# Moving one of the three u-computations of a slot behind the next W1 in a conv + low-rank mixer kernel

## The chip, the cores and the metric

The kernel runs on one core of a Trainium2 chip. The metric is the device time in microseconds of one execution; "before" is the median of three runs. A core has five engines that run side by side and wait for each other with semaphores: TensorE (PE in the profile, its weight loads PEld), VectorE (DVE), ScalarE (ACT), GpSimd (POOL) and SyncE (SP), which here only issues DMAs. TensorE writes its results to PSUM, which has eight banks of 128 x 512 floats; VectorE or ScalarE must copy a result out before its bank can be used again.

## The reference

The input x is 8 x 4224 x 192 (batch, sequence, channel). First comes a causal convolution with 7 taps along the sequence, with one set of taps, after a softmax, for each of 8 heads of 24 channels:

```python
w = np.exp(weight - weight.max(-1, keepdims=True)); w /= w.sum(-1, keepdims=True) + 1e-9
y[b, s, h, g] = sum_k w[h, k] * x_pad[b, s + k, h, g]
```

Then, with y as the x of the mixer:

```python
xt = x.transpose(0, 2, 1)
h = xt @ U @ V                       # rank 32, along the sequence
u = x + h.transpose(0, 2, 1)
ch = np.maximum(u @ w_ch1, 0.0) @ w_ch2   # 192 -> 768 -> 192
return (u + ch).astype(np.float32)
```

U and V mix along the whole sequence of a batch, so nothing of u of a batch can be had before the conv of that batch is done.

## The kernel before, in words

The 8 x 33 tiles of 128 sequence positions are handled in 33 groups of eight tiles (`NG`, `GT`). A group does not respect batches: batch b is tiles 33b to 33b + 32. The steps are:

- **conv** of a batch (`conv32` from batch 2 on, L317; `conv` before, L351): matmuls of x with banded matrices (L335 or L365), head by head, two PSUM banks a head, copied to `y_sb` by `evac` (ScalarE L252, VectorE L254). The string of letters (`AAD`, `AD`) says which engine makes which copy in turn.
- **t** (`tt_mm`, `tt_split`) and **s** (`tt_sum`): y times U, summed, to `tt_sb`.
- **h** of a group (`h_group`, `h_tiles`, L442): eight matmuls of `tt_sb` with V (L453), two tiles of a pair to one PSUM bank, and then on VectorE the adds u = y + h (L475) from PSUM to `u_sb`. A group that starts on an odd tile of its batch, or runs over the edge of two batches, has five banks and six shorter and longer adds rather than four of one kind. Behind the adds, `transp` issues a transposing DMA on SP's queue (L494), which makes `uT` of the group.
- **W1** of a group (`w1`, L538): 36 matmuls (L550) from `uT` with the first weight, six chunks m of two banks each, and behind each chunk two ReLUs out of PSUM to `rl_sb`, on ScalarE (L564) or VectorE (L566): seven and five per group.
- **W2** of two tiles (`w2`, L573; "a pair" below): 12 matmuls (L579) from `rl_sb` with the second weight to one bank, an add of u on VectorE to `out_sb` (L588) and a DMA to the output on SP's queue (L596).

All PSUM tiles come from one pool of eight banks under one tag. `out_sb` has eight buffers, `u_sb` seven, `uT` five.

The order is written out by hand: the kernel runs under a manual schedule, and every engine executes its instructions in the order in which the code issues them. `SLOTS` (L615) is the list of slots, counted from 0 here. A slot is W1 of its groups in the first list, then the W2 pairs of the groups in the second list, four pairs a group; the dictionary says what is done ahead of which pair ("position"; a slot of three groups has positions 0 to 12):

```python
for gs1, gs2, at in SLOTS:
    for g in gs1: ends = w1(g, ...)
    for p in range(npc + 1):
        for what in at.get(p, []): do(what)
        if p < npc: w2(g, 2 * k, 2)
```

From slot 5 on both lists are the same three groups, and in the slot u of three later groups is made. In slots 5 to 9 there is also the conv of a batch (positions 2 to 4 in slot 5, positions 1 to 3 in slots 6 to 9: three heads, three heads, two heads), t and s. Slots 10 to 12 have three h at positions 0, 4 and 8, and slot 13 has none.

GpSimd loads x (L79) during W1 of groups in `LOADS` (L666), held back to chosen W1 matmuls, and makes a shifted copy of x for the conv (`x_shift`, L282: L289, L291 and L301).

Of the kernel before, what the change touches and what calls it, by code (L numbers as in the profile page):

```python
# [14 lines left out]
def kernel(  # L15
# [40 lines left out]
    def bank():  # L56
        return psp.tile([P, 512], F32, name="ps", tag="ps")
# [192 lines left out]
    def evac(eng, out, in_):  # L250
        if eng == "A":
            nc.scalar.activation(out=out, in_=in_, func=ACT.Copy)  # L252
        else:
            nc.vector.tensor_copy(out=out, in_=in_)  # L254
# [27 lines left out]
    def x_shift(b):  # L282


        xbt[b] = xbs.tile([P, NB1, D], BF16, name="xb_sb")

        def same(s0, s1, *rest):
            def step():
                nc.gpsimd.tensor_copy(out=xbt[b][:, s0:s1, :], in_=xt[b][:, s0 + 1 : s1 + 1, :])  # L289
                for t0, t1 in rest:  # L290
                    nc.gpsimd.tensor_copy(  # L291
                        out=xbt[b][HB : HB + QB, t0:t1, :],
                        in_=xt[b][HB : HB + QB, t0 + 1 : t1 + 1, :],
                    )

            return step

        def ahead(r, s0, s1):
            def step():
                q = slice(HB * r + QB, HB * r + HB)  # L300
                nc.gpsimd.tensor_copy(out=xbt[b][q, s0:s1, :], in_=xt[b][q, s0:s1, :])  # L301

            return step

        m = NB0 // 2
        return [
            same(0, m),
            same(m, NB0, (NB0, NB1)),
            ahead(0, 0, m),
            ahead(0, m, NB0),  # L310
            ahead(1, 0, m),
            ahead(1, m, NB1),
        ]
# [3 lines left out]
    def conv32(b, h0, nh, engs):  # L317


        if yt[b] is None:  # L320
            yt[b] = ys.tile([P, NT, D], BF16, name="y_sb")
        nk = (NB0 // 2, NB1 // 2)
        for n in range(nh):
            h = h0 + n
            hs = slice(h * GS, h * GS + GS)
            pp = [bank(), bank()]
            for cg in range(4):
                t, w, st = (
                    (xt[b], bands[h // HQ][:, h % HQ, QB : 2 * QB], 1 + cg // 2)
                    if cg % 2  # L330
                    else (xbt[b], band2[:, h, :], cg // 2)
                )
                for r in range(2):
                    hr = slice(HB * r, HB * r + HB)
                    nc.tensor.matmul(  # L335
                        out=pp[r][QB * cg : QB * cg + QB, 0 : nk[r] * GS],
                        lhsT=w[hr],
                        rhs=t[hr, st : st + 2 * nk[r] - 1 : 2, hs],
                        start=True,
                        stop=True,  # L340
                        tile_position=(HB * r, QB * cg),
                    )
            for part in range(2):
                j0 = NB0 // 2 * part
                evac(
                    engs[(2 * n + part) % len(engs)],
                    yt[b][:, j0 : j0 + nk[part], hs],
                    pp[part][:, 0 : nk[part] * GS].rearrange("p (k a) -> p k a", a=GS),
                )

    def conv(b, h0, nh, rs, engs, k0=0, k1=NT, pp=None):  # L351

        if yt[b] is None:
            yt[b] = ys.tile([P, NT, D], BF16, name="y_sb")
        nk = {r: min(k1, (NB0, NB1)[r] // 2) - k0 for r in rs}
        if pp is None:
            pp = {r: bank() for r in rs}
        w = nh * GS
        for hh in range(nh):
            h = h0 + hh  # L360
            for halo in range(2):
                for r in rs:
                    for c in range(2):
                        st = 1 - halo + c + 2 * k0
                        last = nc.tensor.matmul(  # L365
                            out=pp[r][HB * c : HB * c + HB, 0 : nk[r] * w].rearrange(
                                "p (k a) -> p k a", a=w
                            )[:, :, hh * GS : hh * GS + GS],
                            lhsT=bands[h // HQ][
                                HB * r : HB * r + HB, h % HQ, HB * halo : HB * halo + HB  # L370
                            ],
                            rhs=xt[b][
                                HB * r : HB * r + HB,
                                st : st + 2 * nk[r] - 1 : 2,
                                h * GS : h * GS + GS,
                            ],
                            start=(halo == 0),
                            stop=(halo == 1),
                            tile_position=(HB * r, HB * c),
                        )  # L380
        for n, r in enumerate(rs):
            j0 = NB0 // 2 * r + k0
            evac(
                engs[n % len(engs)],
                yt[b][:, j0 : j0 + nk[r], h0 * GS : h0 * GS + w],
                pp[r][:, 0 : nk[r] * w].rearrange("p (k a) -> p k a", a=w),
            )
        return last
# [95 lines left out]
    def h_group(g):  # L484
        t0, t1 = g * GT, g * GT + GT
        while t0 < t1:
            b = t0 // NT
            te = min(t1, (b + 1) * NT)
            h_tiles(b, t0 - b * NT, te - b * NT)
            t0 = te  # L490

    def transp(g):
        uTt[g] = uts.tile([P, 4, 3, P], BF16, name="uT")
        return nc.sync.dma_start_transpose(  # L494
            out=uTt[g][:].rearrange("p i c t -> p (i c) t"),
            in_=ut[g][:].rearrange("p i c f k -> p (i c f k)"),
        )
# [100 lines left out]
    def held(ins, after):  # L598
        tc.add_manual_dep(
            ins.ins,  # L600
            after.ins.name,
            mybir.DependencyInfo(mybir.DependencyClass.Sync, mybir.DependencyReason.DATA),
            reason="transfer held back",
        )

    def x_load(b, q, after):
        if q == 0:
            x_tile(b)
            x_zero(b, nc.gpsimd)
        held(x_part(b, *XP[q]), after)  # L610
# [17 lines left out]
                6: ["t2"],  # L628
                8: ["s2"],
                9: ["h8"],  # L630
                11: ["h9"],
            },
        ),
    ]
    nh = 10
    for k in range(5, 14):
        gs = list(range(3 * k - 9, 3 * k - 6))
        hs = [f"h{g}" for g in range(nh, min(nh + 3, NG))] + [None] * 3
        nh = min(nh + 3, NG)
        if k == 5:  # L640
            at = {
                2: ["c3:0:3:AAD"],
                3: ["c3:3:3:AAD"],
                4: ["c3:6:2:A", "x4:3"],
                5: [hs[0]],
                6: ["t3"],
                8: ["s3", hs[1]],
                11: [hs[2]],
            }
        elif k < 10:  # L650
            b = k - 2
            at = {
                1: [f"c{b}:0:3:AAD"],
                2: [f"c{b}:3:3:AAD"],
                3: [f"c{b}:6:2:A"] + ([f"x{b + 1}:3"] if b + 1 < B else []),
                5: [f"t{b}", hs[0]],
                7: [f"s{b}"],
                8: [hs[1]],
                11: [hs[2]],
            }  # L660
        else:
            at = {0: [hs[0]], 4: [hs[1]], 8: [hs[2]]}
        SLOTS.append((gs, gs, {p: [w for w in what if w] for p, what in at.items()}))
# [92 lines left out]
    def do(what):  # L756
        if what[0] == "c":
            b, h0, n, engs = what[1:].split(":")
            conv32(int(b), int(h0), int(n), engs)
            return  # L760
        if what[0] == "d":
            for h in range(H):
                last = conv(int(what[1:]), h, 1, [0, 1], "AA" if h == 2 else "AD")
            held(transp(3), last)
            return
        if what[0] == "l":
            b, q = (int(v) for v in what[1:].split(":"))
            x_load(b, q, done_w2[-1])
            return
        if what[0] == "x":  # L770
            b, n = (int(v) for v in what[1:].split(":"))
            steps.extend(x_shift(b))
            for _ in range(n):
                steps.pop(0)()
            return
        n = int(what[1:])
        if what[0] == "h":
            h_group(n)
            if n > 1 and n != 3:
                transp(n)  # L780
        elif what[0] == "t":
            tt_split(n, tt_mm(n, range(NT)))
        else:
            tt_sum(n)
# [55 lines left out]
```

## Time and profile before

| | us |
|---|---|
| runs | 325.15, 325.98, 326.2 (median 325.98) |
| profiled execution | 325.15 |
| its span, first to last instruction | 323.4 |
| granted TensorE clock (share of full speed) | 0.999 |
| PE, DVE, ACT, POOL busy | 318.0, 269.0, 170.5, 143.5 |
| W1 matmuls (L550), ReLUs of ACT and DVE | 131.7; 124.3 and 105.3 |
| W2 matmuls (L579), output adds (L588) | 141.9; 70.3 |
| u adds (L475), 168 instructions | 66.2 |

Where the slots lie, by the start of their W1 in the chain that ended last: slot 4 at 56.4, slot 5 at 81.1, then 109.4, 137.5, 165.8, 193.9, 222.0, 246.9, 271.8, and slot 13 at 296.4 us. A row of a timeline reads: start, duration, engine, line, operation, what it writes and reads, how many instructions are merged in the row, and in brackets the idle time before and what ended it. A row of the chain reads: start, length, and what the end of the kernel hung on in that stretch; "issue" is time for which the profile shows no wait. The duration of a matmul (246 ns of one at L579) is longer than the distance of two of them, since they are pipelined; distances of starts tell the pace.

### The profile page before, as it was taken

The page shows a single profiled execution, that of the slowest core. Times are in us where ns is not written, and L with a number is a line of the kernel's source. Part 1 is how long each engine was busy: PE and PEld are TensorE (multiplying, and loading weights), DVE is VectorE, ACT ScalarE, POOL GpSimd, SP SyncE. Part 2 cuts the span into 40 slices and gives each one's busy share as a digit, 9 for nine tenths or more (in the row PEclk, how much of TensorE's full clock was granted, in tenths as well). Part 3 has the DMA queues.
Part 4 walks back from the last instruction along what each step waited for, and adds up shares of the span by engine and source line. Part 5 has one row for each costly group of instructions (what it writes and reads, how often), then busy time and mean ns, then how long its engine had stood idle before and what let it go on. Part 6 is the DMA issues. An engine that isn't in the chain of part 4 may idle for free.

```text
span 323.4 us, 9590 instructions
## 1 busy us (share of the span) xinstructions
PE 318.0 (98%) x3998; PEld 223.8 (69%) x3998; DVE 269.0 (83%) x551; ACT 170.5 (53%) x344; POOL 143.5 (44%) x112
## 2 busy tenths in 40 slices
PE   8999999999999999999999999999999999999996
PEld 3757676478677647866864784587797497487495
DVE  7769989987977986998798699879888897896864
ACT  1766724860874397088339708824903902912920
POOL 8684179728957694786859489000000000000000
PEclk9999999999999999999999999999999999999999
DMA  9999993999999899699799957139269059048035
GB/s 104 192 192 177 211 213 99 183 196 263 206 126 214 226 176 171 171 152 201 169 240 131 229 160 195 35 111 245 56 168 272 3 149 264 29 121 270 2 119 176
DMA packets 122907, 53.52 MB, mean 166 GB/s; under 512 B 87760, under 2 KB 122832, under 8 KB 122864
## 3 DMA queue, kind: packets, MB, share of 16 engines
q1 hardware_dynamic: 84528, 38.08, 47.5%
q0 software_dynamic: 38192, 14.73, 40.0%
q8 instruction: 31, 0.51, 0.7%
q10 hardware_dynamic: 144, 0.10, 0.1%
q14 instruction: 12, 0.10, 0.1%
HBM read 29.49 MB, written 25.95 MB: 171 GB/s over the span
## 4 chain that ended last, share of the span: by engine, by line
PE 94%; ACT 3%; DVE 2%; issue 0%
PE ps L579 42%; PE ps L550 39%; PE ps L335 3%; PE ps L453 3%; PE ps L155 2%; PE ps L398 2%; ACT rl_sb L564 2%; PE ps L365 1%; ACT y_sb L252 1%; DVE u_sb L475 1%; DVE rl_sb L566 1%; PE ps L520 0%; PE ps L505 0%; DVE band L254 0%; PE ps L678 0%; PE ps L424 0%
## 5 line engine op out<-in xcount | busy, mean ns | idle before, releaser
L564 ACT ACTIVATE rl_sb<-ps 128x512 bf16<-128x512 f32 x233 | 124.3, 604 | 108.0 <-PE ps L550 96.0
L579 PE MATMUL ps<-W_sb,rl_sb 128*128 128x192 bf16 x1584 | 141.9, 246 | 0.2
L579 PEld LDWEIGHTS <-rl_sb 128*128 128x128 bf16 x1584 | 128.1, 98 | 13.5 <-issue 13.1
L550 PE MATMUL ps<-uT,W_sb 64*128 64x512 bf16 x1188 | 131.7, 376 | 0.0
L566 DVE TENSOR_SCALAR rl_sb<-ps 128x512 bf16<-128x512 f32 x163 | 105.3, 687 | 15.7 <-PE ps L550 15.4
L550 PEld LDWEIGHTS <-W_sb 64*128 64x128 bf16 x1188 | 66.8, 94 | 60.6 <-issue 3.8
L588 DVE TENSOR_TENSOR out_sb<-ps,u_sb 128x384 f32<-128x384 f32 (+1 forms) x133 | 70.3, 548 | 25.9 <-PE ps L579 25.5
L301 POOL COPY xb_sb<-x_sb 32x3072 bf16<-32x3072 bf16 (+1 forms) x24 | 67.5, 2824 | 0.7
L475 DVE TENSOR_TENSOR u_sb<-y_sb,ps 128x192 bf16<-128x192 bf16 (+1 forms) x168 | 66.2, 459 | 0.0
L289 POOL COPY xb_sb<-x_sb 128x3072 bf16<-128x3072 bf16 x12 | 32.7, 2742 | 36.2 <-DMA x_sb<-in_x_dram 22.3
L252 ACT ACTIVATE y_sb<-ps 128x384 bf16<-128x384 f32 (+4 forms) x90 | 38.2, 515 | 10.4 <-PE ps L335 7.8
L79 POOL DMA_DIRECT2D x_sb<-in_x_dram x32 | 27.0, 848 | 17.2 <-PE ps L550 10.3
L254 DVE CAST y_sb<-ps 128x408 bf16<-128x408 f32 (+4 forms) x36 | 19.2, 577 | 0.8 <-PE ps L365 0.7
L453 PE MATMUL ps<-tt_sb,V_sb 32*128 32x192 bf16 x264 | 12.4, 246 | 0.1
L335 PE MATMUL ps<-xb_sb,band 64*32 64x384 bf16 x192 | 12.1, 332 | 0.0
L335 PE MATMUL ps<-x_sb,band 64*32 64x384 bf16 x192 | 12.1, 333 | 0.0
L453 PEld LDWEIGHTS <-V_sb 32*128 32x128 bf16 x264 | 4.7, 92 | 7.3 <-issue 7.3
L155 PE MATMUL ps<-zz 128*128 128x512 f32 x12 | 7.6, 786 | 1.5 <-DVE zz L145 1.5
L365 PE MATMUL ps<-x_sb,band 64*64 64x240 bf16 (+3 forms) x192 | 7.9, 276 | 0.4 <-DVE band L254 0.4
L412 ACT ACTIVATE tt_hi<-ps 128x192 bf16<-128x192 f32 x8 | 2.6, 330 | 10.6 <-PE ps L398 10.5
L335 PEld LDWEIGHTS <-band 64*32 64x32 bf16 x384 | 4.5, 89 | 4.1 <-issue 3.0
L365 PEld LDWEIGHTS <-band 64*64 64x64 bf16 x192 | 5.9, 106 | 2.2 <-issue 1.2
(65 smaller groups left out, 72.7 us busy)
## 6 DMA issues: line engine op xcount, KB each, us to landing
out_dram<-out_sb SPq DMA_DIRECT2D x131, 192.0 KB, 2.8
x_sb<-in_x_dram POOLq DMA_DIRECT2D x14, 384.0 KB, 7.8
x_sb<-in_x_dram POOLq DMA_DIRECT2D x7, 432.0 KB, 8.5
x_sb<-in_x_dram POOLq DMA_DIRECT2D x7, 408.0 KB, 9.0
x_sb<-in_x_dram POOLq DMA_DIRECT2D x1, 504.0 KB, 7.4
uT<-u_sb SPq DMA_TRANSPOSE x31, 3.7
x_sb<-in_x_dram POOLq DMA_DIRECT2D x1, 480.0 KB, 5.7
W_sb<-in_moe_w_ch_dram POOLq DMA_DIRECT2D x2, 192.0 KB, 7.6
```

What stands on the lines that cost most here:

```text
L79: return nc.gpsimd.dma_start(out=xt[b][HB * r : HB * r + HB, s0:s1, :], in_=x[b, blk * HB : (blk + s1 - s0) * HB, :].rearrange("(j p) d -> ...
L252: nc.scalar.activation(out=out, in_=in_, func=ACT.Copy)
L289: nc.gpsimd.tensor_copy(out=xbt[b][:, s0:s1, :], in_=xt[b][:, s0 + 1 : s1 + 1, :])
L301: nc.gpsimd.tensor_copy(out=xbt[b][q, s0:s1, :], in_=xt[b][q, s0:s1, :])
L335: nc.tensor.matmul(out=pp[r][QB * cg : QB * cg + QB, 0 : nk[r] * GS], lhsT=w[hr], rhs=t[hr, st : st + 2 * nk[r] - 1 : 2, hs], start=True, ...
L453: nc.tensor.matmul(out=banks[pr][:, a * D : (a + 1) * D], lhsT=V_sb[32 * q : 32 * q + 32, (j // 8) * 2 + j % 2, :], rhs=ttb[b][32 * q : 32 ...
L475: nc.vector.tensor_tensor(out=u_group(g)[:, i : i + n, :, hf, :], in0=yt[b][:, run[0] : run[0] + n, :].rearrange("p n (c k) -> p n c k", c=3),
L550: last = nc.tensor.matmul(out=pps[m][hf][:], lhsT=W1_sb[HB * hf : HB * hf + HB, c, m * P : (m + 1) * P], rhs=uTt[g][HB * hf : HB * hf + HB ...
L564: nc.scalar.activation(out=rl[:, m, hf, :], in_=pp[hf][:], func=ACT.Relu)
L566: nc.vector.tensor_scalar_max(out=rl[:, m, hf, :], in0=pp[hf][:], scalar1=0.0)
L579: last = nc.tensor.matmul(out=cps[:, a * D : (a + 1) * D], lhsT=rlt[g][:, m, hf, (i + a) * P : (i + a + 1) * P], rhs=W2_sb[:, m, :], start ...
L588: nc.vector.tensor_tensor(out=o[:, 0:n, :].rearrange("p n (c k) -> p n c k", c=3), in0=cps[:, 0 : n * D].rearrange("p (n c k) -> p n c k", ...
```

## The change

Three edits:

1. In slots 5 to 9 the three h stood at positions 5, 8 and 11. Now h stand at 0, 5 and 8, and the groups shift by one: what was the third h of a slot is the first of the next, right behind its W1. h9, at position 11 of slot 4, goes to position 0 of slot 5.
2. In slots 10 to 12 the positions stay 0, 4 and 8, but by the shift slot 10 has h24, h25, h26 in place of h25, h26, h27, and so on; slot 12 has a third h, h32, at position 8, where it had none.
3. In the conv of batch 1 (slot 2, step `d1`), the second copy of head 2 goes from ScalarE to VectorE, so that each engine makes eight of sixteen.

The amount of work is the same; a transposing DMA goes with each h that moves.

```diff
@@ SLOTS, slot 4
                 9: ["h8"],
-                11: ["h9"],
             },
         ),
     ]
-    nh = 10
+    nh = 9
     for k in range(5, 14):
         gs = list(range(3 * k - 9, 3 * k - 6))
         hs = [f"h{g}" for g in range(nh, min(nh + 3, NG))] + [None] * 3
@@ if k == 5
                 4: ["c3:6:2:A", "x4:3"],
-                5: [hs[0]],
+                0: [hs[0]],
+                5: [hs[1]],
                 6: ["t3"],
-                8: ["s3", hs[1]],
-                11: [hs[2]],
+                8: ["s3", hs[2]],
             }
         elif k < 10:
             b = k - 2
             at = {
+                0: [hs[0]],
                 1: [f"c{b}:0:3:AAD"],
                 2: [f"c{b}:3:3:AAD"],
                 3: [f"c{b}:6:2:A"] + ([f"x{b + 1}:3"] if b + 1 < B else []),
-                5: [f"t{b}", hs[0]],
+                5: [f"t{b}", hs[1]],
                 7: [f"s{b}"],
-                8: [hs[1]],
-                11: [hs[2]],
+                8: [hs[2]],
             }
         else:
             at = {0: [hs[0]], 4: [hs[1]], 8: [hs[2]]}
@@ do, "d"
             for h in range(H):
-                last = conv(int(what[1:]), h, 1, [0, 1], "AA" if h == 2 else "AD")
+                last = conv(int(what[1:]), h, 1, [0, 1], "AD")
             held(transp(3), last)
```

## The prediction, made before the result was known

> **What bounds the kernel now.** I read the page's table of engines, then the chain that ended last in order of time, then the timelines of PE and DVE around three places. "Slot n" counts SLOTS from 0; T is the moment PE leaves the slot's last W1 matmul.
>
> ```profile
> PE 318.0 (98%) x3998; PEld 223.8 (69%) x3998; DVE 269.0 (83%) x551; ACT 170.5 (53%) x344; POOL 143.5 (44%) x112
> ```
>
> PE never rests for long, so each microsecond that PE waits in the middle of the kernel is a microsecond at the end. What matters is therefore not how much DVE does, but where PE has to wait for it. The chain shows one such place, in slot 4, the only conv slot with an h straight behind W1 (h7 at position 0):
>
> ```profile
> 63.31 1.78 DVE rl_sb L566 x3
> 65.09 0.12 issue
> 65.22 0.83 DVE u_sb L475 x3
> 66.05 0.16 issue
> 66.21 1.07 DVE u_sb L475 x3
> 67.28 0.48 DVE out_sb L588
> 67.76 0.04 issue
> 67.80 1.15 PE ps L579 x12
> ```
>
> For 4.5 us the chain runs over DVE: last ReLUs of W1, six adds of h, the first output add, and only then PE may start its next W2 pair. Slot 6 of the same kernel has no h there and the chain stays on PE:
>
> ```profile
> 107.99 0.35 PE ps L453 x8
> 108.34 1.10 PE ps L579 x12
> 109.44 11.76 PE ps L550 x108
> 121.20 1.10 PE ps L579 x12
> 122.30 0.64 PE ps L335 x19
> 122.94 1.10 PE ps L579 x12
> 124.04 0.71 PE ps L335 x17
> ```
>
> This is h12 before the last W2 pair, that pair, W1, a W2 pair, three heads of conv (0.64 us when nothing holds them), a pair, three heads (0.71, of which 0.07 is a wait for a ScalarE copy). Slots 10 to 12 already start with an h; there it is followed by four W2 pairs and no conv:
>
> ```profile
> 246.88 11.76 PE ps L550 x108
> 258.64 0.45 PE ps L453 x8
> 259.08 4.07 PE ps L579 x48
> ```
>
> The pace of DVE behind W1, from its timeline in slots 4 and 10:
>
> ```profile
> 65.22 2.06 DVE L475 TENSOR_TENSOR u_sb<-y_sb,ps 128x192 bf16<-128x192 bf16 x6
> 67.20 1.01 DVE L588 TENSOR_TENSOR out_sb<-ps,u_sb 128x384 f32<-128x384 f32 x2
> 234.49 1.94 DVE L475 TENSOR_TENSOR u_sb<-y_sb,ps 128x384 bf16<-128x384 bf16 x4
> ```
>
> The adds begin at T + 0.72 (PE's h starts at 64.50, the adds at 65.22; the same in slots 10 to 12: 0.71, 0.74, 0.74), because three ReLUs of W1 are still to do. A two-tile add lasts 0.545 us and the next starts 0.465 after it, a one-tile add 0.344 and 0.265; these give back the 1.94 of four long ones and the 2.06 of two long and four short.
>
> **The rule of the banks.** PSUM tiles come from one ring of eight. After W1 the ring's next banks are those of m2, m3, m4, m5 (two each). An h takes four (five if its eight tiles start in the middle of a pair), a W2 pair one, a head of conv two. Slot 4 proves the ring: h7 takes five, two pairs two, and the third head needs the last bank of h7: PE's third head stands in two parts there, 67.20 and 67.34, the sixth add ending at 67.28. The next pair takes the bank of the first pair, freed at 67.75 by DVE, and starts at 67.80. From the release of a bank to PE's start it is 0.05.
>
> **Part 1: conv of batch 1, one copy from ScalarE to DVE.** PE's timeline there:
>
> ```profile
> 37.75 3.24 PE L365 MATMUL ps<-x_sb,band 64*64 64x384 bf16 x64
> 40.93 0.64 PE L453 MATMUL ps<-tt_sb,V_sb 32*128 32x192 bf16 x8
> 41.61 1.15 PE L579 MATMUL ps<-W_sb,rl_sb 128*128 128x192 bf16 x12
> ```
>
> DVE does seven copies in 3.51 us from 38.50, one each 0.49; ScalarE nine in 3.59 from 38.35. With eight, DVE's copies of heads 3 to 7 end 0.49 later. h1 behind the conv takes the banks of heads 4 and 5; DVE frees head 5's at 41.51 instead of 41.03, while before it was ScalarE's copy of head 5 (41.17) that held h. So h's second half starts at about 41.57 instead of 41.22 and the W2 pair, until now held to 41.61 by ScalarE's copy of head 6, at 41.76: **+0.15** (between -0.2, were only ScalarE's hold on 41.61 to go, and the whole 0.49). DVE is late afterwards but has 0.15 to 0.43 us idle before each of the next output adds; PE next needs the low half of the sum at 45.53, and DVE, which delivers at 44.59 now, delivers at 45.08.
>
> **Part 2: no h before W1 in slots 4 to 9.** DVE then reaches W1 without six adds behind it. The W1 stages after such an h last 11.83, 11.76, 11.91, 11.76, 11.76 and 11.83 us (slots 5 to 10); those of slots 11 to 13, with none, 11.76. Gain **-0.29**; 11.76 also stands where nothing delays DVE, so there is no more to have.
>
> **Part 3: the h matmuls themselves.** No h is added or taken away; eight now stand at position 0 (h9, h12, h15, h18, h21, h24, h27, h30). A five-bank h there takes 0.46 (slots 11 and 12: 0.45, 0.47), since its fifth bank still holds a ReLU of ScalarE; a four-bank one 0.28 (slot 10). Five-bank are h12, h15, h21, h24, h30. After: 5 x 0.46 + 3 x 0.28 = 3.14; the same eight before: 0.35 twice, 0.28 six times = 2.38. h28 and h31 leave position 0 for position 4: 0.92 becomes 0.56. Sum 0.76 - 0.36 = **+0.40**. With each h its transposing DMA moves on SP's queue: in slots 5 to 9 it stands before the first output write of the slot instead of before the last. It waits for the h adds, which come before that output add on DVE anyway, so the writes behind it lose only the transpose's issue of some 1.3 to 2.7 us; eight output buffers stand for over 8 us of pairs. Its result is wanted by a W1 one slot (some 28 us) later; h26, h29 and h32, now at position 8, are wanted third in the next W1, four pairs and two W1 groups (4.4 + 7.8 us) on, the lead that h11 and its like have already. POOL's queue is unchanged in order. Cost 0; if uncovered, the price is a rival below.
>
> **Part 4: the conv behind the h, slots 5 to 9.** Times from T. Slots 6, 7 and 9 (five banks): h to 0.46, pair to 1.56, conv. Head 1 takes m5; head 2 takes the h's banks 1 and 2 (free at 1.55 at the latest), head 3 banks 3 and 4, the next pair bank 5. Adds from 0.74 with two long and four short: bank 4 free at 2.54, bank 5 at 2.80. Head 3 therefore resumes at 2.59 and the pair, 0.30 behind (122.56 to 122.87), starts at 2.89; without a wait it would be 1.56 + 0.64 = 2.20. **+0.69 each**. Slot 8 (h18, four banks, long adds): unhindered pair at 0.28 + 1.10 + 0.64 = 2.02; its bank is the h's fourth, free at 2.65, so 2.70: **+0.68**. Slot 5 has its conv at position 2: conv at 2.37, pair at 3.01; that pair takes the first pair's bank, freed by the output add at 2.56 + 0.55 = 3.11, so 3.16: **+0.15**. Sum 3 x 0.69 + 0.68 + 0.15 = **+2.90**. What follows is later by as much and finds its copies done, so the 0.07 in the second block of heads goes: 5 x 0.07 = **-0.35**. From below, the nearest row is slot 4 itself, where two pairs stand between and the block takes 0.93 instead of 0.64: 0.29 x 4 + 0.15 = 1.3. From above, DVE's delay of some 2 us per slot shows whole: the second block waits as long again as slot 4's, 2.90 + 5 x 0.29 = 4.35. I take 2.90, because the ring reproduces slot 4 to 0.01 us.
>
> One rule speaks against this part. The Trainium skill (Perfetto Trace Analysis, Matmuls) says that independent groups rotating through different banks let the evacuation of one overlap the matmuls of the next. By it Part 4 would cost nothing, and the sum would be -0.09. The row at 67.28 to 67.80 above shows a rotation of eight that is too short behind W1, and I go by the row.
>
> **Sum:** 0.15 - 0.29 + 0.40 + 2.90 - 0.35 = **+2.81 us**. The profiled execution took 325.15 us (span 323.4 and 1.75 around it), the lowest of three; +2.81 gives 327.96. On the median of 325.98 it is **328.8 us**, 0.9% slower. A measurement of this kernel tells about 0.3%, 1 us, from no change.
>
> **Rivals.**
> *Faster: the ends of slots gain and the conv does not pay.* If DVE were through with the h before the third head needs its banks, the -0.29, -0.35 and -0.36 stay and only 0.15 is paid: -0.85, 325.1 us, just under the 0.3%. It needs the adds to begin at about T rather than T + 0.72. For it: W1 of slot 7 does lose 0.15 to an h before it. Against it: all four places with an h behind W1 show 0.71 to 0.74. It decides when Part 4 and the 0.46s cost less than 0.85 together.
> *No change: the wait is that of slot 5 everywhere.* 5 x 0.15 = 0.75 for Part 4: the sum is 0.66, 326.6 us. For it: the longer slot 4 block cost 0.29 only. Against it: there two pairs, 2.09 us, stand between h and conv, in slots 6 to 9 one.
> *Slower still: the moved transpose collides with the loads of x.* In slots 6 to 8 the four x loads are issued during W1, the last about 12 us in (121.48), and take 7.8 to 9.0 us; the transpose now falls among them instead of before them. POOL's second shifted copy starts at 129.2, about when that load lands. Delayed by one whole transpose (3.7 us), POOL's copies end late by what is not covered by its idle time before the next x load (2.33, 3.12 and 3.21), by the 0.68 from the last copy's end (121.55) to the conv, and by the 0.28 or more that the h adds in front: 3.7 - 2.33 - 0.68 - 0.28 = 0.4, so at most about 0.5 per slot, 1.5 in three, 330.3 us. For it: the page's DMA row is at 9 in most slices up to 200 us. Against it: in slots 6 and 7 POOL's wait is for the conv (126.45, 154.65), not for a load.
>
> **How the numbers follow.** Forecast 0.80, slower still 0.08, no change 0.07, faster 0.05. Low end: Part 4 at 1.3 gives +1.21, 327.2. High end: Part 4 at 4.35 gives +4.26, 330.2, with the collision's 330.3 beside it. So 327.2 to 330.3, which leaves out the no-change and the faster case. Slower by over 0.3%: 0.80 + 0.08, same 0.07, faster 0.05 (its 325.1 is near the bound).
>
> **What would show it.** In the changed kernel's chain: every W1 of slots 5 to 13 at 11.76; in slots 6 to 9, behind the first pair, pieces of DVE u_sb L475, and a first conv block 1.3 us long rather than 0.64, the second 0.64; slot 5's first block 0.79; slots 10 to 12 together unchanged within 0.1 us; the pair behind h1 at 41.76. Slots 6, 7 and 9 should grow by 0.5 to 0.8 us, slot 8 by 0.6. The prediction is wrong if the first blocks keep 0.64 (the ring is not what holds them), or if conv waits for xb_sb (the collision).

## The result

The changed kernel takes 327.4 us (median of six runs, 327.03 to 328.26) against 325.12 us of the kernel before in six runs (324.99 to 326.2): ratio 1.0065, 95% interval 1.0045 to 1.0085, 2.3 us slower. Measured a second time it was 327.25 us against 324.95: 1.0075, 1.0051 to 1.0100. The ratios and their intervals are estimated from the runs of both kernels without the few slow ones, so they need not equal the quotient of the two medians. The profiled execution took 327.47 us with a span of 325.7, which is 2.3 us over the 323.4 of before.

The page says little. PE's line, as the other engines', is nearly that of before:

```profile
PE 319.6 (98%) x3998; PEld 216.0 (66%) x3998; DVE 270.4 (83%) x552; ACT 170.1 (52%) x343; POOL 143.5 (44%) x112
```

The chain that ended last, in slot 6, shows where time was lost and where it was won (start, length, what the end hung on):

```profile
105.24 4.07 PE ps L579 x48
109.31 11.76 PE ps L550 x108
121.07 0.47 PE ps L453 x8
121.54 1.10 PE ps L579 x12
122.64 0.37 PE ps L335 x5
123.00 0.49 ACT y_sb L252
123.49 0.04 issue
123.53 0.36 PE ps L335 x5
123.89 1.10 PE ps L579 x12
124.99 0.64 PE ps L335 x19
125.63 1.10 PE ps L579 x12
126.73 0.47 PE ps L335 x11
```

The last four pairs before W1 now run through (4.07). Behind W1 stands h12 with 0.47 us, then one pair, then the first conv block: from 122.64 to 123.89 it takes 1.25 us instead of 0.64. The second block has lost its small wait (0.64 instead of 0.71). DVE and ACT in the same place, from their timelines:

```profile
121.75 2.06 DVE L475 TENSOR_TENSOR u_sb<-y_sb,ps 128x384 bf16<-128x384 bf16 x6
123.73 0.55 DVE L588 TENSOR_TENSOR out_sb<-ps,u_sb 128x384 f32<-128x384 f32 x1
```

```profile
122.99 1.68 ACT L252 ACTIVATE y_sb<-ps 128x384 bf16<-128x384 f32 x4 [1.27 <-PE ps L335]
```

The six adds start 0.75 us after PE leaves W1 (121.00 in PE's timeline) and are still going on when the third head asks for its banks. The chain hangs on ScalarE's copy of head 1, not on an add: the third head's second bank is the one that head 1 has just used. Slots 7 and 9 show the same (ACT y_sb on the chain at 151.68 and 208.94). In slot 8, with the four-bank h18, it hangs on the adds:

```profile
180.11 0.56 DVE u_sb L475
180.67 0.04 issue
180.71 0.36 PE ps L335 x5
181.07 1.10 PE ps L579 x12
```

Slot 11, whose h at position 0 is now four-bank, has it for 0.28 where it was 0.45:

```profile
248.98 11.76 PE ps L550 x108
260.74 0.28 PE ps L453 x8
```

And the place of edit 3, in PE's timeline:

```profile
37.91 3.37 PE L365 MATMUL ps<-x_sb,band 64*64 64x384 bf16 x64
41.22 0.28 PE L453 MATMUL ps<-tt_sb,V_sb 32*128 32x192 bf16 x3
41.73 0.32 PE L453 MATMUL ps<-tt_sb,V_sb 32*128 32x192 bf16 x5 [0.23 <-DVE y_sb L254]
41.98 1.16 PE L579 MATMUL ps<-W_sb,rl_sb 128*128 128x192 bf16 x12
```

h1's second half waits for a VectorE copy of the conv, as said. Everything in this profile starts 0.16 us later than in that of before (the first W1 at 20.61 against 20.45), so the pair at 41.98 is 0.21 late by the edit.

The slots by the distance of their first W1 matmuls in PE's timeline:

| slot | 4 | 5 | 6 | 7 | 8 | 9 | 10 | 11 | 12 |
|---|---|---|---|---|---|---|---|---|---|
| before | 24.73 | 28.30 | 28.05 | 28.27 | 28.13 | 28.12 | 24.87 | 24.95 | 24.61 |
| after | 24.35 | 28.16 | 28.68 | 28.76 | 28.50 | 28.69 | 25.04 | 24.79 | 24.98 |

"PE's way" below is the time from the first W1 matmul to the first matmul of the last W2 stage: 287.68 us before and 289.83 after. In the second profile of the changed kernel it is 289.84. What lies ahead of it and behind it is not steady: over the twelve profiles of this study the first W1 starts between 20.2 and 21.5 us, and the last stage takes 15.2 to 16.4 us to the end of the span.

### The profile page after: what moved, and what is told of

The parts are those of the page before. It is cut to its first block, busy times and chain, and to the rows that moved or that the text cites. A ratio compares the mean times of both kernels' runs of the same rounds, so it can differ in the third digit from the quotient of the medians.

```text
span 325.7 us, 9590 instructions
## 1 busy us (share of the span) xinstructions
PE 319.6 (98%) x3998; PEld 216.0 (66%) x3998; DVE 270.4 (83%) x552; ACT 170.1 (52%) x343; POOL 143.5 (44%) x112
## 4 chain that ended last, share of the span: by engine, by line
PE 91%; DVE 6%; ACT 1%; issue 1%
PE ps L579 40%; PE ps L550 38%; PE ps L453 3%; PE ps L335 3%; PE ps L155 2%; DVE rl_sb L566 2%; PE ps L398 2%; DVE u_sb L475 2%; PE ps L365 1%; ACT rl_sb L564 1%; DVE y_sb L254 1%; PE ps L520 0%; ACT y_sb L252 0%; PE ps L505 0%; DVE out_sb L588 0%
## 5 line engine op out<-in xcount | busy, mean ns | idle before, releaser
L579 PEld LDWEIGHTS <-rl_sb 128*128 128x128 bf16 x1584 | 128.3, 98 | 11.1 <-issue 10.2
L566 DVE TENSOR_SCALAR rl_sb<-ps 128x512 bf16<-128x512 f32 x163 | 106.7, 689 | 20.8 <-PE ps L550 20.5
L550 PEld LDWEIGHTS <-W_sb 64*128 64x128 bf16 x1188 | 58.3, 94 | 68.8 <-issue 2.9
L252 ACT ACTIVATE y_sb<-ps 128x408 bf16<-128x408 f32 (+4 forms) x89 | 37.8, 513 | 14.3 <-PE ps L335 12.5
L335 PE MATMUL ps<-xb_sb,band 64*32 64x384 bf16 x192 | 13.7, 332 | 0.4
```

The lines of the kernel that those rows point to most:

```text
L335: nc.tensor.matmul(out=pp[r][QB * cg : QB * cg + QB, 0 : nk[r] * GS], lhsT=w[hr], rhs=t[hr, st : st + 2 * nk[r] - 1 : 2, hs], start=True, ...
L550: last = nc.tensor.matmul(out=pps[m][hf][:], lhsT=W1_sb[HB * hf : HB * hf + HB, c, m * P : (m + 1) * P], rhs=uTt[g][HB * hf : HB * hf + HB ...
L566: nc.vector.tensor_scalar_max(out=rl[:, m, hf, :], in0=pp[hf][:], scalar1=0.0)
L579: last = nc.tensor.matmul(out=cps[:, a * D : (a + 1) * D], lhsT=rlt[g][:, m, hf, (i + a) * P : (i + a + 1) * P], rhs=W2_sb[:, m, :], start ...
```

## The experiments

In the diffs and profile rows, `...` stands for code or rows that are left out. The lines of the diffs are those of slots 6 to 9 where `b` stands in them; slot 5, where it is named too, gets the same positions.

**Edit 3 alone** (kernel before, with it).

```diff
-                last = conv(int(what[1:]), h, 1, [0, 1], "AA" if h == 2 else "AD")
+                last = conv(int(what[1:]), h, 1, [0, 1], "AD")
```

> The kernel before with edit 3 alone (the second copy of head 2 of the conv of batch 1 on VectorE). Theory: this edit costs PE a wait at h1 behind that conv, read in the changed kernel's chain as a start of the W2 pair 0.2 us later than its start-up alone explains. So +0.2 us, ratio 1.0006, and the h matmuls behind the conv stretched. If the prediction's 0.15 is the size, +0.15. Rival: the chain's whole +0.39 us at the start of slot 4 is this edit, +0.4 us, ratio 1.0012. The slots from 4 on keep their lengths of the kernel before under both.

PE's way is 287.90 us, +0.22, and all slots from 4 on are those of before to 0.01 us. PE's timeline has the picture of the changed kernel:

```profile
40.84 0.28 PE L453 MATMUL ps<-tt_sb,V_sb 32*128 32x192 bf16 x3
41.36 0.32 PE L453 MATMUL ps<-tt_sb,V_sb 32*128 32x192 bf16 x5 [0.23 <-DVE y_sb L254]
```

So the edit costs 0.2 us, not 0.15 and not 0.4. The time measured is more: 326.45 us against 325.61, ratio 1.0032 (1.0017 to 1.0047). The rest, 0.6 us, is not on PE's way: in the profile the last stage takes 16.02 us instead of 15.25, and the start is 0.21 earlier. Whether that is chance or follows from the edit is open; the changed kernel, which has the same edit, has 15.25 there in both of its profiles.

**The h alone** (changed kernel without edit 3).

```diff
-                last = conv(int(what[1:]), h, 1, [0, 1], "AD")
+                last = conv(int(what[1:]), h, 1, [0, 1], "AA" if h == 2 else "AD")
```

> The changed kernel without edit 3: only the h are moved. Theory: the loss sits in the first conv blocks of slots 5 to 9 (1.83 + 0.54 + 0.19 = 2.56 us over the three-head 0.64), with 0.51 for h at position 0, less 0.29 in W1, less 0.35 in the second conv blocks, less 0.55 for pairs no longer split by an h: +1.9 us, ratio 1.0058. Rival, edit 3 carries 0.4 or more of the loss: below +1.7, ratio under 1.0052.

PE's way is 289.60, +1.92, as expected; the slots from 4 on are those of the changed kernel to 0.01 us. The time is 327.69 us, ratio 1.0076 (1.0055 to 1.0097): the expected 1.0058 lies inside the interval, the rival's value, under 1.0052, outside it. So 1.92 of the 2.15 us on PE's way come from the moved h.

**The conv later** (changed kernel; slots 5 to 9).

```diff
                 0: [hs[0]],
-                1: [f"c{b}:0:3:AAD"],
-                2: [f"c{b}:3:3:AAD"],
-                3: [f"c{b}:6:2:A"] + ...
-                5: [f"t{b}", hs[1]],
-                7: [f"s{b}"],
-                8: [hs[2]],
+                3: [f"c{b}:0:3:AAD"],
+                4: [f"c{b}:3:3:AAD"],
+                5: [f"c{b}:6:2:A"] + ...
+                7: [f"t{b}", hs[1]],
+                9: [f"s{b}", hs[2]],
```

> The changed kernel with, in slots 5 to 9, the conv at positions 3, 4 and 5, t and the second h together at 7, s and the third h together at 9; the first h stays right behind W1. Theory: with three W2 pairs between that h and the conv, VectorE has made its adds when the conv asks for banks, so the first conv block falls back to 0.64 us (gain 2.56 on the changed kernel), and five splits of W2 pairs fewer gain 0.5: 3.1 us faster than the changed kernel, 0.8 us faster than before, ratio 0.9975. Rival one, the h behind W1 is dear in itself whatever follows: the blocks stay above 1 us and the ratio stays at 1.004 or more. Rival two, the loads and the transposes collide: the ratio stays near 1.006, or POOL's copies come late and conv waits for xb_sb.

The blocks do what the theory says, the sum does not. In slot 6:

```profile
121.22 0.47 PE ps L453 x8
121.69 3.08 PE ps L579 x36
124.76 0.64 PE ps L335 x19
...
133.37 1.07 DVE u_sb L475 x3
134.45 0.48 DVE out_sb L588
134.92 0.04 issue
134.97 1.07 PE ps L579 x11
```

With three pairs between, the first block is 0.64 in all five slots: the h behind W1 is not dear in itself. But PE's way is 288.79, only 1.04 us shorter than the changed kernel's, because the third h, now two pairs behind the second, is stretched in slots 6, 8 and 9 to 0.80, 0.67 and 0.80 us: its banks are those of the second h, whose adds VectorE has not finished. It is the same wait in another place. The second blocks also take 0.71 again. Nor does it gain to put an h next to s: the pairs run through, but s with an h behind it takes 0.26 instead of 0.16. The time is 327.73 us, ratio 1.0063 (1.0049 to 1.0077), 1.0 us over what PE's way gives; in its profile the last stage takes 16.42.

**The second h next to s** (kernel before; slots 6 to 9).

```diff
-                7: [f"s{b}"],
-                8: [hs[1]],
+                7: [f"s{b}", hs[1]],
```

> The kernel before with the second h of slots 6 to 9 at position 7, next to s, in place of position 8. Theory of the split: twelve W2 matmuls cost 1.10 us as a pair by itself but 0.99 as the continuation of another (24 take 2.09, 36 take 3.08 in the chain), so each place where something stands between two pairs costs 0.11 us; here four such places fall together with another: -0.44 us, ratio 0.9986. Rival: the 0.11 us is only how the chain books the start of a stage, and the time is unchanged.

Slower: 326.72 us against 325.61, ratio 1.0032 (1.0014 to 1.0050). Four pairs now take 4.05 to 4.07 where a single one and three took 1.09 and 3.08, so the 0.11 is real; s gives 0.10 of it back, and in slots 6, 8 and 9 the h takes 0.80, 0.67 and 0.80 us, two pairs behind another. Slots 6 to 9 are 1.17 us longer in sum, about the 1.11 between the medians. (The profile is of the slowest run, 329.05 us; its other loss, 2.1 us in slots 4 and 5, comes behind an output write that took 8.89 us.) The gain of an unsplit run of pairs is only had where the h goes to a border that is there anyway and VectorE is not late.

**The transposes later** (changed kernel; the five transposes of position 0 issued at position 4).

```diff
-                4: ["c3:6:2:A", "x4:3"],
+                4: ["c3:6:2:A", "x4:3", "T9"],
...
+                4: ["T" + hs[0][1:]],
...
+    LATE = (9, 12, 15, 18, 21)
...
-            if n > 1 and n != 3:
+            if n > 1 and n != 3 and n not in LATE:
                 transp(n)
+        elif what[0] == "T":
+            transp(n)
```

> The changed kernel, with the transposing DMA of the five h that stand behind W1 in slots 5 to 9 issued at position 4 in place of position 0; their matmuls and adds stay. Theory (VectorE and the banks): the first conv blocks keep 1.26, 1.26, 1.19 and 1.26 us in slots 6 to 9 and the slots keep the changed kernel's lengths to 0.1 us; the time is the changed kernel's, ratio 1.006 to 1.007. Rival (the moved transposes collide with the x loads on the DMA queues): the blocks and slots shorten, ratio 1.004 or less.

PE's way is 289.83 and all slots are those of the changed kernel to 0.02 us, with the same chain in slot 6:

```profile
122.27 0.36 PE ps L335 x5
122.64 0.49 ACT y_sb L252
123.12 0.04 issue
123.17 0.36 PE ps L335 x5
```

The time is 327.19 us (327.03 to 327.64) against 325.86 us of before in that session, ratio 1.0042 (1.0023 to 1.0060). By time alone that lies between the two theories; the profile decides: where the transposes are issued is not what costs.

**A first block of two heads** (changed kernel; slots 6 to 9).

```diff
-                1: [f"c{b}:0:3:AAD"],
-                2: [f"c{b}:3:3:AAD"],
-                3: [f"c{b}:6:2:A"] + ...
+                1: [f"c{b}:0:2:A"],
+                2: [f"c{b}:2:3:AAD"],
+                3: [f"c{b}:5:3:AAD"] + ...
```

> The changed kernel with the conv of slots 6 to 9 in blocks of two, three and three heads in place of three, three and two (the two-head block wholly copied by ScalarE, as before). Theory: it is the third head that finds no free bank, so a first block of two heads takes 0.47 to 0.6 us, the pair behind it waits 0.1 to 0.2 for an add of h, and slots 6 to 9 shorten by 0.4 to 0.6 us each: ratio about 1.000 to 1.002. Rival, the wait is for something that a block of any size must wait out (the copy of x, the transposes, ScalarE's late start): the first block or the pair behind it stays as long, ratio 1.006.

```profile
121.35 1.09 PE ps L579 x12
122.44 0.50 PE ps L335 x11
...
122.95 1.16 PE ps L579 x12
```

The first block takes 0.58, 0.57, 0.47 and 0.57 us from its start to the next pair, slots 6 to 9 shorten by 0.44 to 0.47, and PE's way is 288.02 us, 1.81 shorter. The time is 325.84 us against 325.86 of before, ratio 1.0001 (0.9980 to 1.0022). What was changed is which head stands on which side of a W2 pair, and with it which engine makes which copy: those of the first block are now all ScalarE's. In the changed kernel VectorE's first copy of the block starts at 124.20, after the third head has both of its banks (123.53), so it was not that copy that held PE. It is the third head, without a bank, that made the loss, and 1.81 of 2.15 us can be given back without moving the h.

**Three attempts at a version that beats both.** All are the changed kernel without edit 3, with h at position 0 and the conv at 3, 4, 5 in slots 5 to 9, and the other two h three positions apart.

The first, in slots 5 to 9 and in slot 4:

```diff
-                5: [f"t{b}", hs[1]],
-                7: [f"s{b}"],
-                8: [hs[2]],
+                7: [f"t{b}", hs[1]],
+                9: [f"s{b}"],
+                10: [hs[2]],
...
-                2: ["c2:0:3:AAD"],
-                3: ["c2:3:3:AAD"],
-                4: ["c2:6:2:A", "x3:4"],
-                6: ["t2"],
-                8: ["s2"],
-                9: ["h8"],
+                3: ["c2:0:3:AAD"],
+                4: ["c2:3:3:AAD"],
+                5: ["c2:6:2:A", "x3:4"],
+                7: ["t2"],
+                9: ["s2"],
+                10: ["h8"],
```

> The changed kernel without edit 3, with the conv three W2 pairs behind the h in slots 4 to 9 (positions 3, 4, 5), t at 7 with the second h, s at 9 and the third h at 10, three pairs behind the second. Theory: first conv blocks 0.64 us in slots 4 to 9 and no h stretched behind s (it was 0.80, 0.67 and 0.80 where only two pairs stood between two h, for want of VectorE), so PE's way from the first W1 to the end of the last one is that of the kernel e3_conv_later less 0.22 (edit 3), 1.43 (the stretched h) and 0.30 (slot 4): 286.8 us against 287.7 of before, a ratio of 0.997 if start and end of the program are as before. Rival, something else than VectorE's backlog stretches: the slots stay longer than those of before and the ratio is over 1.

In slots 5 to 9 it went as expected (27.94, 28.13, 28.21, 28.02, 28.14 us, 0.43 less than before in sum). But here slot 4 also had its conv one pair later, and in the profiled execution (328.58 us) the chain there runs over a late output:

```profile
70.87 8.64 DMA out_dram<-out_sb
```

An output write took 8.6 us, VectorE waited for its buffer, and PE for VectorE: slot 4 took 27.98 us. Time 325.86 against 325.86, single runs from 324.56 to 331.69, ratio 1.0022 (0.9990 to 1.0053). The DMA share (the packets' time over that of 16 engines) is 1.22 in slot 4 of this profile and 1.04 in slot 5; but it is 1.27 in slot 4 of the kernel before, where VectorE waits for no output write. The profile of the kernel with h next to s, whose slot 4 was not edited, had such a wait there too. So what makes a write late is not shown, and the conv's new place in slot 4 is not shown to be the cause.

The second is the first without the edit of slot 4.

> The kernel e6_both_apart with slot 4 left as in the changed kernel (conv at position 2, h8 at 9). Theory: slots 5 to 9 as there (27.9 to 28.2 us), slot 4 24.4 us without a late output, so the way from the first W1 to the last W2 stage is 0.4 us shorter than in the kernel before; ratio 0.9985, and never 328 us or more. Rival: the late outputs of slot 4 have to do with the whole order and not with the conv's place in slot 4, and single runs of 328 us and more stay.

The rival's mark appeared: runs of 329.4, 329.6 and 330.8 us stayed. In the profile slot 4 is 24.36 us, but slot 7 is 28.81, since the third group of W1 waits for its transpose:

```profile
137.90 0.57 PE ps L550 x5
138.47 7.68 DMA uT<-u_sb
```

The h at position 10 is two pairs and two W1 groups ahead of that, some 10 us, and its transpose falls among the x loads. Time 325.59 against 325.81, ratio 1.0012 (0.9980 to 1.0045).

The third, from the second:

```diff
-                5: [f"c{b}:6:2:A"] + ...
-                7: [f"t{b}", hs[1]],
-                9: [f"s{b}"],
-                10: [hs[2]],
+                5: [f"c{b}:6:2:A"] + ... + [hs[1]],
+                7: [f"t{b}"],
+                8: [hs[2]],
+                9: [f"s{b}"],
```

> The kernel e8_slot4_kept with, in slots 5 to 9, the second h at position 5 behind the last conv block, t at 7, the third h at 8 as in the changed kernel, and s at 9. Theory: the third W1 group of e8 waited because an h at position 10 sends its transpose among the x loads (landing 7.7 us); at position 8 it lands in 4 to 5 us before them, so no W1 stage is over 11.76 us and no run is at 328 us or more; the first conv blocks stay at 0.64, so the way from the first W1 to the last W2 stage is about 287.3 us against 287.7 of before: ratio 0.998 to 0.999, at the edge of what can be told. Rival, the spread of e6 and e8 has another cause: runs of 328 us and more stay.

Worse: 328.01 us against 324.95, ratio 1.0079 (1.0063 to 1.0094). Two things. The last conv block is copied by ScalarE alone, and the h behind it waits for those copies (0.50 or 0.90 instead of 0.28, in all five slots). Slots 5 to 9 have 2.3 us of this in sum. And in this profile, of the slowest of the seven runs (330.53 us), a load of x came late, so that POOL's copies came late and the conv of slot 6 waited for them:

```profile
96.63 13.42 DMA x_sb<-in_x_dram
...
124.43 3.09 POOL xb_sb L301
127.52 0.04 issue
127.56 0.71 PE ps L335 x16
```

No version was found that is clearly faster than the kernel before.

**The changed kernel once more**, unedited.

> The changed kernel once more, on the chip of e9_h_after_conv. Theory: ratio 1.006 within 0.002, the way from the first W1 to the last W2 stage 289.8 us, as its first profile has it, since that way is set by waits between instructions and not by chance.

It was as expected (1.0075, PE's way 289.84).

## Why the prediction was right, and where its sum was off

It said 328.8 us (327.2 to 330.3) and +2.81; measured are 327.4 us and +2.3. Of the 1.4 us between 328.8 and 327.4, 0.9 is the base: it started from 325.98, the median of three runs, and six runs give 325.12. So 327.4 lies just inside the low end of the range, while +2.3 as a change lies well inside the +1.21 to +4.26 that the range was made of. The direction, the place and the shortage of banks were right. That the sum came within 0.7 us of PE's way is in part luck, since terms that were too small (Parts 1 and 3, 0.18 together) offset some of those that were too large or not counted (0.29 and 0.57). By its own terms, measured from the stages of the two profiles:

| term | said | measured |
|---|---|---|
| Part 1, edit 3 | +0.15 | +0.23 |
| Part 2, W1 without an h before it | -0.29 | -0.29 |
| Part 3, h matmuls | +0.40 | +0.50 |
| Part 4, first conv blocks, slots 5; 6, 7, 9; 8 | 0.15 + 3 x 0.69 + 0.68 = +2.90 | 0.20 + 3 x 0.62 + 0.55 = +2.61 |
| Part 4, second blocks | -0.35 | -0.35 |
| runs of W2 pairs no longer split | not there | -0.57 |
| PE's way | +2.81 | +2.13 (read directly: +2.15) |

With the start, 0.16 us later in the changed kernel's profile than in that of before, the two spans differ by 2.3.

- **The missing term.** The prediction counted h stages and took them as moved at their own length. It did not count what a stage does to the pairs on both sides. In the kernel before, the pairs at the end of slot 6 are three and one around h15 (before's chain has the like in slot 5, where the single pair, quoted in the prediction, takes 1.10):

```profile
104.92 3.08 PE ps L579 x36
```

  3.08 + 1.10 is 4.18; after, four in one run take 4.07. Six places fall away (slots 4 to 9) and one is new (h32 in slot 12, 8.03 to 8.14): -0.68 + 0.11. At position 0 PE changes from W1 to another kind of matmul anyway. The numbers stood in the lines that the prediction quotes: 1.10 for one pair, and 4.07, not 4.40, for four. The Trainium skill (TensorEngine Tiling (Array Packing), Tiling Modes) says that a change of the tiling mode drains TensorE; W1 uses rows in halves, h in quarters and W2 whole, and the runs here agree, with 0.11 us for the split of a run of pairs.
- **Part 4: right shortage, partly the wrong bank.** The order of banks is not simply the ring of eight. The built program has for slot 6 banks 0, 7, 3, 6, 2 for the h in the order of its adds, 1 for the pair, 5 and 4 for head 1, 0 and 7 for head 2, and for head 3 banks 3 and 5: the second is head 1's own, and not 6. So PE resumed with the end of ScalarE's copy at 123.49 and not with an add (the matmuls that start at 123.53 wait for ScalarE's semaphore alone, and the add on bank 6 ends only at 123.55), and the pair, on bank 6, was not held by the fifth bank: 2.83 after the start of h instead of 2.89. In slot 8 the pair takes head 1's bank, not the fourth of h: 2.57 instead of 2.70. This is 0.34 of the 2.90, less 0.05 the other way in slot 5, whose block waits for the first output add, as said. That the size still came near is luck: the copy that did end the wait and the add that was to end it lie 0.07 us apart. Slot 4, on which the rule was proved, does not tell the two orders apart.
- **Part 1 and Part 3** were a little low: 0.21 to 0.23 us, since the conv itself also waits (3.30 instead of 3.17 to h1); and h24 takes 0.53, not 0.46.
- **What was to be seen.** Right: W1 at 11.76 everywhere, first blocks of 1.26, second ones of 0.64, slots 6, 7 and 9 longer by 0.63, 0.49 and 0.57 (0.5 to 0.8 was said). Wrong: u_sb of VectorE on the chain of slots 6, 7 and 9 (there it is y_sb of ScalarE), slot 5's first block (0.84, not 0.79), the pair behind h1 (41.98, or 41.82 without the late start, not 41.76), slot 8 (+0.37, not 0.6), and slots 10 to 12 "unchanged": they are 0.38 longer together, since slot 12 has an h more and slot 10 a five-bank one.
- **Rivals.** The faster case and the case of no change fell with the first blocks, which are 0.55 to 0.62 us longer in slots 6 to 9 where they allowed 0.15 at most. No collision of the moved transposes was found in the changed kernel; the prediction had the order the wrong way round. Those of position 11 fell among the x loads, those of position 0 behind most of them. (That rival's 7.8 to 9.0 us for an x load are medians over the whole program; in slots 6 to 8 of before's profile the loads take 5.9 to 10.5.) From issue to landing, the page's kind of row for the stretch of each, h12, h15 and h18, before and then after:

```profile
uT<-u_sb SPq DMA_TRANSPOSE x1, 7.9
uT<-u_sb SPq DMA_TRANSPOSE x1, 9.5
uT<-u_sb SPq DMA_TRANSPOSE x1, 9.7
```

```profile
uT<-u_sb SPq DMA_TRANSPOSE x1, 4.4
uT<-u_sb SPq DMA_TRANSPOSE x1, 4.3
uT<-u_sb SPq DMA_TRANSPOSE x1, 4.4
```

  The latter vary from execution to execution (6.9, 6.1 and 4.4 in the profile without edit 3). Nobody waits for them in either kernel. The weighed rule, that rotating banks hides the evacuation, failed here with 0.55 to 0.62 us a slot in slots 6 to 9, and held again with a head fewer in front (0.47 to 0.58) or two pairs more (0.64).

## What to carry to other kernels

An engine that is off the chain sets PE's pace through the buffers that it holds: before moving VectorE work next to a stage that takes many PSUM banks at once, write down bank by bank when each comes free, from the built program rather than from an assumed order. Count a move's border effects as well, since what stands between two runs of one kind of matmul costs more than its own length. And where the ends of a program vary by a microsecond from run to run, compare the stretch between them, which here repeats to 0.02 us.

## What the runs showed of the hardware that was not expected

- PE's way from the first W1 to the last stage is the same to 0.01 us in three profiles with the changed kernel's order of matmuls (289.83 and 289.84, on at least two chips), while over all twelve profiles the start varies by 1.3 us and the last stage by 1.2 us.
- A transposing DMA of one group lands in 3.2 us at best (as in slots 10 to 13, where no x is loaded), and in 7.7 to 10.2 us from position 11 of slots 5 to 7, where it goes out among the loads of x (three profiles). An output write, usually 2.8 us (median), took 8.6 and 8.9 us on the chain of two profiles in slot 4; one of 8.7 us in slot 8 of the kernel before held nobody up.
